# One plain run of 18 steps around the second norm, and whole tiles for the products of the FFN

## The chip, the cores and the metric

The kernel runs on one core of a Trainium2 chip. The metric is the device time of one execution in microseconds. A profiled execution also has a span, from its first to its last instruction, which lies a little below its time.

## The reference

One transformer block over 2048 rows of width 512, in float32. The vector `c` gives six modulation vectors. The block is attention with 32 heads of width 16, then a SwiGLU FFN of inner width 1792, each behind a normalization without weights.

```
mod = (_silu(c) @ w_mod).reshape(c.shape[0], 6, 1, -1)
sa, ca, ga, sb, cb, gb = (mod[:, 0], mod[:, 1], mod[:, 2], mod[:, 3], mod[:, 4], mod[:, 5])
h = _layernorm(x, axis=-1) * (1 + ca) + sa
x = x + ga * _A_ref(h, A_wqkv, A_wo)
h = _layernorm(x, axis=-1) * (1 + cb) + sb
x = x + gb * _B_ref(h, B_w_gate, B_w_up, B_w_down)
```

`_A_ref` is softmax attention over all 2048 keys followed by the product with `wo`; `_B_ref` is `(silu(x @ w_gate) * (x @ w_up)) @ w_down`.

## The kernel before

The 2048 rows are four **chunks** of 512 queries, the 32 heads eight groups of four. A chunk with a group is a **unit** of attention, 32 in all, chunk by chunk; a unit has 16 **steps**, one for each block of 128 keys, so there are 512 steps. The first three chunks (0 to 2) run the rest of their block (output product, second norm, FFN) while the attention of the next chunk goes on; the last chunk's rest comes behind all attention. The change touches the part in which both run.

A step is four **pairs** (`pair_of`). A pair is a score matmul (`score`, L573), whose result ScalarE turns into exponentials (L575), and a matmul for the row maxima of the keys of 20 steps later (`max_one`, L524), whose result VectorE reduces (L526). The two matmuls of a pair use the two row halves of TensorE. Every 16 steps a unit's maxima are complete; they are then written as two extra rows into its `qop`, with which the first score of that unit, 16 pairs later, is made. That is done in one of two ways. `max_rows` reduces (L531), makes three small matmuls (L536 to L538) two windows later and sends two DMAs (L542). `max_turned` reduces (L549), works on VectorE (L554, L556) and sends eight small DMAs on SyncE's queue (L563); its parts are hung, one each, behind the next five pairs. The flag `beside` says which: false in plain runs, true in tiles.

The product of exponentials and values, PV, comes in halves of a step (`pv_step`, L588), made in groups by `pvs`, one step behind the scores. After the last half of a unit, `close_unit` sends its sums on and loads keys and queries for the unit three later.

TensorE's order is written out by two functions:

- `plain(steps, tails)` runs pairs without FFN work. A **window** is three pairs, then a tail if there is one for this window, then one or two PV halves after the pattern `HALVES`, then the work whose turn in the list `behind` has come (`turns_behind` counts down once a window). The maxima take turns on four PSUM banks; a tail takes one of the same four. Each call begins that order of banks anew.
- `filled_tile(job, ...)` puts the matmuls of an FFN product between pairs. With the order `FOUR`, 16 pairs and all 24 pieces of work are one stretch, behind which all PV halves follow; the product's row halves then trade banks in the middle. Where the tile would start on a unit's last step (`one` is false), it is cut into two calls with the order `TWO`, eight pairs each and its own PV group behind each. A down product (`DOWN`) is eight pairs.

For chunk `ci` the program is: plain up to step `STARTS[ci]`; the two output products; the norm run; 14 gate-and-up tiles (`gate_up`) and 14 down tiles (`down`) in the order of `ch.jobs`. The norm run begins with the sums of the second norm on ScalarE (`minus_mean` L829, `squares` L833), put into `behind` by `add_o`; then `scaled` (three VectorE operations, L746 to L748, 13 small GpSimd ones and four normalizing ones, L768); then four tails `ch.turned` (four transposes L773 into one bank, evacuated by ScalarE in L775, split by GpSimd in L776 and L777), whose results the first gate tile reads. Before the change the run is `plain(9)` with tails in its last three windows and `plain(3)` with the fourth in its first; chunk 2 adds 18 plain steps there and six before its gate tile 7. Chunks 0 and 1 have three plain steps ahead of their last pair of down tiles, (6, 0) and (6, 2). What remains up to the next `STARTS` is plain. Weights come on SyncE's queue, one gate weight of 1 MB for each tile (L718) and one down weight of 1 MB for each pair of tiles (L723).

Of the kernel before, what the change touches and what calls it, by code (L numbers as in the profile page):

```python
# [28 lines left out]
NK = D // P  # L29
# [4 lines left out]
NF = F // P  # L34
FG = 2
# [6 lines left out]
WIN = 3  # L42
# [3 lines left out]
PTS = 5  # L46
FBANKS = (3, 6)
KEEP = 7
REST = 18
NORM = 9  # L50
STARTS = (147, 275, 403)
TWO = (0, 3, 2, 2, 2, 2, 1, 0)
DOWN = (0, 3, 3, 0, 3, 3, 0, 0)
# [51 lines left out]
def block_kernel(ctx, tc, x, wqkv, wo, w_gate, w_up, w_down, c, w_mod, out):  # L105
# [391 lines left out]
    posts, behind = [], []  # L497
# [134 lines left out]
    def tile_mid():  # L632
        return pf.tile([P, 2, CW], F32R, name="mid", tag="mid", bufs=3)

    def tmp(name):
        return pf.tile([P, CW], F32, name=name, tag="tmp", bufs=4)
# [177 lines left out]
    def add_o(ch, t0, outs, late):  # L814
        if ch.mv is None:
            ch.mv = pf.tile([P, 4, 2], F32, name="mv2", tag="mv2", bufs=1)
            ch.rs = pf.tile([P, 4], F32, name="rs", tag="rs", bufs=1)
            ch.rs2 = pf.tile([P, 2, 4], F32, name="rs2", tag="rs2", bufs=1)
        for e in range(2):
            t = t0 + e  # L820
            nc.vector.tensor_add(ch.x2[:, t, :], outs[e], ch.x2[:, t, :])

        def sums(t):
            st = pf.tile([P, 6], F32, name="stt", tag="stt", bufs=2)
            nc.vector.bn_stats(st, ch.x2[:, t, :])
            nc.vector.bn_aggr(ch.mv[:, t, :], st)

        def minus_mean(t):
            nc.scalar.activation(tmp("sq"), ch.x2[:, t, :], AF.Identity, scale=-1.0 / D,  # L829
                                 accum_out=ch.mv[:, t, 0:1])  # L830

        def squares(t):
            nc.scalar.activation(tmp("sq"), ch.x2[:, t, :], AF.Square, bias=ch.mv[:, t, 0:1],  # L833
                                 accum_out=ch.mv[:, t, 1:2])

        if late:
            turns = (1, 1, 2, 2) if t0 == 0 else (1, 2, 3, 4)
            works = ((minus_mean, t0), (squares, t0), (minus_mean, t0 + 1), (squares, t0 + 1))
            behind.extend([k, lambda f=f, t=t: f(t)] for k, (f, t) in zip(turns, works))
        else:  # L840
            for e in range(2):
                sums(t0 + e)

    def out_pair(ch, t0, outs, halves, trade=False):
        return accumulate(outs, lambda e, a, k: ch.oT[a][:, k, (t0 + e) * P:(t0 + e + 1) * P],
                          lambda b, k: ch.wo[k // 2][:, b, k % 2, :], NK,
                          lambda: posts.append(lambda: add_o(ch, t0, outs, True)), halves, trade=trade)
# [60 lines left out]
    def scaled(ch):  # L908
        ch.load_gu(0)
        ch.norm_scale(nc.gpsimd)  # L910
        ch.nt = [tile_mid().bitcast(F32) for _ in range(2)]
        for t in range(4):
            ch.normalize(t)
# [40 lines left out]
    beside = True  # L954
# [28 lines left out]
    def pair_of():  # L983
        nonlocal done
        i = done // 4 - 1
        most = 4 * n - 4 * (LEAD - 1)
        h = (ORDER if done < most else (0, 1, 2, 3))[done % 4]
        work = [lambda: score(i + 1, h)]
        if done < most:
            work.insert(1 - h % 2, lambda: max_one(done + 4 * (LEAD - 1)))  # L990
        for f in work:
            f()
        done += 1
        if side:
            side.pop(0)()
# [22 lines left out]
    def pvs(most, by_halves):  # L1018

        nonlocal owed  # L1020
        if by_halves:
            most, owed = most + owed, 0
        while most and halves and 4 * halves[0][0] + 8 <= done:
            i, half = halves.pop(0)
            pv_step(i, half)
            most -= 1
            if i % 16 == 15 and half:
                close_unit(i // 16, done // 4 - 1)
                if by_halves:
                    break  # L1030
        if by_halves and most and halves and 4 * halves[0][0] + 8 <= done:
            owed = most

    def turns_behind():
        for b in list(behind):
            b[0] -= 1
            if not b[0]:
                b[1]()
                behind.remove(b)

    def end_steps():
        nonlocal ended
        while ended < done // 4:
            after(ended - 1)
            ended += 1

    def plain(steps, tails=()):

        nonlocal four, bank, beside
        beside = False  # L1050
        assert steps % WIN == 0 and done % 4 == 0
        four, bank = Turn(0, 3, 1, 2), Turn(4, 5, 6)
        for w in range(4 * steps // WIN):
            for _ in range(WIN):
                pair_of()
            if w < len(tails) and tails[w]:
                tails[w](four())
            pvs((HALVES[(w - 2) % 4] if done > 8 else 0) + (w == 4 * steps // WIN - 1), True)
            turns_behind()
            end_steps()  # L1060

    def filled(places, work):

        nonlocal four, bank, beside
        beside = True
        four, bank = three, Turn(4, 5)
        if done >= 4 * n - 4 * (LEAD - 1):
            places, bank = ALONE.get(places, places), Turn(4, 5, 0, 1, 2)
        for r in range(len(places)):
            pair_of()  # L1070
            take(work, places[r])
            if r % 4 == 3:
                end_steps()
        hook()
        pvs(len(places) // 2 + 2, False)
        turns_behind()

    def filled_tile(job, ch, arg):
        one = done // 4 % 16 != 15 and done + 16 <= 4 * n - 4 * (LEAD - 1)
        work = job(ch, arg, outs, True, one)  # L1080
        for places in (FOUR,) if one else (TWO, TWO):
            filled(places, work)
# [14 lines left out]
    for ci in range(last):  # L1097
        plain(STARTS[ci] - done // 4)
        ch = chunks[ci]
        for t0 in (0, 2):  # L1100
            filled_tile(out_pair, ch, t0)
        behind.append([4, lambda: scaled(ch)])
        tails = [lambda tp, k=k: ch.turned(tp, k) for k in range(NK)]
        plain(NORM, [None] * NORM + tails[:3])
        plain(WIN, tails[3:])
        if ci == last - 1:
            plain(REST)
        for _ in range(len(ch.jobs) - (KEEP if ci == last - 1 else 0)):
            job, args = ch.jobs.pop(0)
            if args == (NF // FG - 1, 0):  # L1110
                plain(WIN)
            if ci == last - 1 and args == (7,):
                plain(24 - REST)
            if job is gate_up:
                filled_tile(job, ch, *args)
            else:
                filled(DOWN, job(ch, *args, outs, True))
# [5 lines left out]
    turns = chain([2, 3, 2, 0, 1, 2, 0], cycle([1, 3, 2, 0]))  # L1123
# [19 lines left out]
    ch, chp = chunks[last], chunks[last - 1]  # L1143
# [10 lines left out]
    for t in range(4):  # L1154
        out_terms(ch, t, banks[t], (NK - 1,))
        if t % 2:
            add_o(ch, t - 1, banks[t - 1:t + 1], False)
# [40 lines left out]
```

## Time and profile before

| | before |
|---|---|
| time, median of 3 runs | 1821.43 us (1820.22 to 1823.81) |
| time of the profiled execution | 1822.87 us |
| its span | 1821.1 us |
| granted clock of TensorE, mean | 0.999 |
| costliest VectorE line, L526 | 1259.7 us busy, 2048 reduces |
| chain that ended last | PE 96%, DVE 2%, ACT 2% |

The busy shares of the page are averages over the whole span, and matmul ends are modelled, so TensorE's share says little about a single stretch. The view of windows gives the busy time and the number of instructions of each engine within chosen stretches; the timeline lists an engine's instructions in order, merged where they follow each other, with the idle time before them and its releaser in brackets.

### The profile page before, as it was taken

What the parts mean: (1) busy time and instruction counts of PE and PEld (TensorE: products, weight loads), DVE (VectorE), ACT (ScalarE), POOL (GpSimd) and SP (SyncE); (2) the same over time, 40 slices, a digit from 0 to 9 for tenths busy, and PEclk for the clock granted to TensorE, in tenths of its full rate; (3) what the DMA queues carried; (4) which work ended last, traced back from release to release, by engine and by line L of the source; (5) the groups of instructions that cost most, each with busy time, mean ns of one, the idle gap of its engine ahead of it and who ended that gap; (6) DMA issues with size and microseconds to landing.
All of it is one profiled execution on the core that took longest, in us unless ns stands there. A gap on an engine that the chain in (4) does not pass through costs nothing.

```text
span 1821.1 us, 41022 instructions
## 1 busy us (share of the span) xinstructions
PE 1809.9 (99%) x16898; PEld 1181.1 (65%) x16898; DVE 1507.0 (83%) x2556; ACT 1234.9 (68%) x2357; POOL 459.9 (25%) x538
## 2 busy tenths in 40 slices
PE   9999999999999999999999999999999999999999
PEld 6876444444455777776565777776564677667887
DVE  5568999999999888888999888888989988922544
ACT  4222888888888666767888676676888867773211
POOL 3612544456323111111123111111113111031200
PEclk9999999999999999999999999999999999999999
DMA  8873866666845444553554554444643565233742
GB/s 290 306 220 133 208 182 201 167 178 192 217 81 124 106 114 141 125 149 69 136 122 109 129 130 119 126 119 89 163 80 57 126 149 121 106 122 118 286 167 103
DMA packets 80596, 267.63 MB, mean 147 GB/s; under 512 B 19744, under 2 KB 24320, under 8 KB 59728
## 3 DMA queue, kind: packets, MB, share of 16 engines
q1 hardware_dynamic: 61432, 179.71, 34.0%
q0 software_dynamic: 18288, 84.49, 19.5%
q8 instruction: 133, 2.18, 0.5%
q10 hardware_dynamic: 688, 0.80, 0.1%
q14 instruction: 55, 0.45, 0.1%
HBM read 201.85 MB, written 62.13 MB: 145 GB/s over the span
## 4 chain that ended last, share of the span: by engine, by line
PE 96%; DVE 2%; ACT 2%; DMA 0%; issue 0%; SPq 0%; DVEq 0%; ACTq 0%
PE bank L588 26%; PE bank L790 20%; PE bank L573 18%; PE bank L524 15%; PE bank L809 8%; PE bank L214 7%; DVE mx L526 2%; PE bank L852 1%; PE bank L773 0%; DMA wm_ab<-in_w_mod 0%; PE bank L166 0%; ACT sq L833 0%; PE bank L538 0%; DVE v_flat L883 0%; PE bank L537 0%
## 5 line engine op out<-in xcount | busy, mean ns | idle before, releaser
L526 DVE TENSOR_REDUCE mx<-bank 128x1 f32<-128x512 f32 x2048 | 1259.7, 680 | 118.4 <-PE bank L524 84.8
L573 PE MATMUL bank<-qop,kop 50*128 50x512 f32 x2048 | 732.2, 427 | 0.6 <-ACT pu__17793 L575 0.2
L524 PE MATMUL bank<-kop,qop 48*128 48x512 f32 x2048 | 726.3, 425 | 0.3
L573 PEld LDWEIGHTS bank<-qop,kop 50*128 50x128 f32 x2048 | 345.5, 184 | 192.0 <-issue 37.4
L524 PEld LDWEIGHTS bank<-kop,qop 48*128 48x128 f32 x2048 | 345.2, 184 | 107.3 <-DVE mx L526 62.5
L790 PE MATMUL bank<-act,wgu 64*128 64x512 f32 x1872 | 306.6, 392 | 0.0
L790 PEld LDWEIGHTS bank<-act,wgu 64*128 64x128 f32 x1872 | 194.0, 187 | 17.6
L614 POOL TENSOR_TENSOR rb<-o,rb 128x512 f32<-128x512 f32 x31 | 39.9, 1286 | 539.1 <-DMA rb<-d_dr 363.2
L790 PE MATMUL bank<-wd,mid 64*128 64x512 f32 x912 | 131.5, 391 | 0.0
L871 POOL CAST mid<-m 128x512 fp32r<-128x512 f32 x40 | 24.4, 611 | 347.6 <-DVE m L869 347.6
L790 PEld LDWEIGHTS bank<-wd,mid 64*128 64x128 f32 x912 | 91.3, 186 | 11.9
L214 PE MATMUL bank<-hT,wqs 128*128 128x512 f32 x384 | 94.5, 397 | 0.6 <-DVE wqs L354 0.4
L214 PEld LDWEIGHTS bank<-hT,wqs 128*128 128x128 f32 x384 | 70.6, 188 | 19.4 <-issue 3.1
L867 DVE SCALAR_TENSOR_TENSOR q<-th,bank 128x512 f32<-128x512 f32 x56 | 38.1, 680 | 54.2 <-ACT th L863 54.2
L863 ACT ACTIVATE th<-bank 128x512 f32<-128x512 f32 x56 | 33.4, 597 | 57.9 <-PE bank L809 57.9
L883 DVE TENSOR_TENSOR x<-bank,x 128x512 f32<-128x512 f32 x84 | 53.9, 685 | 16.2 <-PE bank L790 16.1
L869 DVE TENSOR_TENSOR m<-bank,q 128x512 f32<-128x512 f32 x56 | 38.7, 692 | 21.7 <-PE bank L809 19.7
L872 POOL TENSOR_TENSOR mid<-m,mid 128x512 fp32r<-128x512 f32 x40 | 51.4, 1285 | 3.3
L809 PE MATMUL bank<-wd,mid 128*128 128x512 f32 x216 | 51.3, 393 | 0.0
L214 PE MATMUL bank<-wqs,hT 128*128 128x512 f32 x192 | 47.9, 397 | 0.0
L790 PE MATMUL bank<-wgu,act 64*128 64x512 f32 x288 | 47.8, 392 | 0.0
L809 PEld LDWEIGHTS bank<-wd,mid 128*128 128x128 f32 x216 | 40.4, 188 | 8.9
(6300 smaller groups left out, 5142.7 us busy)
## 6 DMA issues: line engine op xcount, KB each, us to landing
wgu<-gu_dr SPq DMA_DIRECT2D x48, 1024.0 KB
wd<-wd_dr SPq DMA_DIRECT2D x28, 1024.0 KB
kop<-kd SPq DMA_DIRECT2D x33, 768.0 KB
kop<-kd POOLq DMA_DIRECT2D x29, 768.0 KB, 8.6
gu_dr<-wgu POOLq DMA_DIRECT2D x14, 1024.0 KB, 12.7
kd<-prt SPq DMA_DIRECT2D x16, 512.0 KB
qd<-prt SPq DMA_DIRECT2D x16, 512.0 KB
kop<-gu_dr SPq DMA_DIRECT2D x8, 1024.0 KB
```

The lines of the kernel that those rows point to most:

```text
L214: nc.tensor.matmul(pt, lhs(a, k), rhs(b, k), start=(n == 0), stop=(n == 3 * nk - 1))
L524: nc.tensor.matmul(pm, qop[u][rows, s, qt * P:(qt + 1) * P], kop[u % 3][rows, s, kc * CW:(kc + 1) * CW], start=True, stop=True)
L526: nc.vector.tensor_reduce(mx[u][:, b, s, qt, kc:kc + 1], pm, op=ALU.max, axis=AX.X)
L573: nc.tensor.matmul(sp, kop[u % 3][rows, h // 2, kt * P:(kt + 1) * P], qop[u][rows, h // 2, :], start=True, stop=True)
L588: nc.tensor.matmul(pv[u][32 * h:32 * h + 32, cols], v_flat[:, e0:e0 + 32], p_[h][:, cols], start=(kt == 0 and half == 0), stop=(kt == 15), ...
L614: mul.tensor_mul(rb, o, rb)
L790: mm = nc.tensor.matmul(outs[e], lhs(e, a, k)[rows], rhs(b, k)[rows], start=(ph == 0 and j == 0), stop=(j == z and (ph == 1 or trade)), sk ...
L809: nc.tensor.matmul(outs[e], lhs(e, a, k), rhs(b, k), start=(j == 0), stop=(j == z))
L867: nc.vector.scalar_tensor_tensor(q, th, 1.0, outs[0], op0=ALU.add, op1=ALU.mult)
L869: nc.vector.tensor_mul(m32, outs[1], q)
L872: (nc.gpsimd if slow else nc.vector).tensor_sub(mid[:, 1, :], m32, mid[:, 0, :].bitcast(F32))
L883: nc.vector.tensor_add(ch.x2[:, t, :], outs[e], ch.x2[:, t, :])
```

## The change

The 9 and 3 steps of the norm run, with tails in windows 9, 10, 11 and 12, become one call of 18 steps (24 windows) with tails in windows 10, 13, 16 and 19, counted from 0. The second output product's sums come in windows with other counts, and `scaled` waits six turns in place of four. The three steps ahead of the last down tiles are gone. Chunk 2's extra steps are 12 in place of 18, so that its norm run and extra steps are 30 in all as before. The runs that lead to `STARTS` shrink by themselves, from 21 to 18 steps. In the last two windows of a plain call `beside` is true.

```diff
-REST = 18
-NORM = 9
+REST = 12
+NORM = 18
...
-            turns = (1, 1, 2, 2) if t0 == 0 else (1, 2, 3, 4)
+            turns = (1, 1, 2, 2) if t0 == 0 else (1, 1, 2, 4)
...
         for w in range(4 * steps // WIN):
+            beside = w > 4 * steps // WIN - 3
...
-        behind.append([4, lambda: scaled(ch)])
-        tails = [lambda tp, k=k: ch.turned(tp, k) for k in range(NK)]
-        plain(NORM, [None] * NORM + tails[:3])
-        plain(WIN, tails[3:])
+        behind.append([6, lambda: scaled(ch)])
+        tails = [None] * 10
+        for k in range(NK):
+            tails += [lambda tp, k=k: ch.turned(tp, k), None, None]
+        plain(NORM, tails)
         if ci == last - 1:
             plain(REST)
...
-            if args == (NF // FG - 1, 0):
-                plain(WIN)
             if ci == last - 1 and args == (7,):
-                plain(24 - REST)
+                plain(18 - REST)
```

How the instructions stand now is shown at three places. The first is ScalarE in the norm run of chunk 0, from the first tail to the third before, and from the first to the second now; L775 evacuates a tail's bank, L575 makes one pair's exponentials. Before:

```order
L775 ACTIVATE h_6596<-bank_64,modc 128x512
L575 ACTIVATE pt__6611<-bank_68 128x512
L575 ACTIVATE pu__6616<-bank_69 128x512
L575 ACTIVATE pt__6619<-bank_67 128x512
L775 ACTIVATE h_6628<-bank_64,modc 128x512
L575 ACTIVATE pt__6640<-bank_68 128x512
L575 ACTIVATE pt__6647<-bank_69 128x512
L575 ACTIVATE pu__6652<-bank_67 128x512
L775 ACTIVATE h_6659<-bank_64,modc 128x512
```

The same place on ScalarE now:

```order
L775 ACTIVATE h_6620<-bank_66,modc 128x512
L575 ACTIVATE pt__6632<-bank_68 128x512
L575 ACTIVATE pt__6639<-bank_69 128x512
L575 ACTIVATE pu__6644<-bank_67 128x512
L575 ACTIVATE pt__6651<-bank_68 128x512
L575 ACTIVATE pt__6656<-bank_69 128x512
L575 ACTIVATE pt__6663<-bank_67 128x512
L575 ACTIVATE pu__6672<-bank_68 128x512
L575 ACTIVATE pt__6675<-bank_69 128x512
L575 ACTIVATE pt__6680<-bank_67 128x512
L775 ACTIVATE h_6689<-bank_65,modc 128x512
```

Nine pairs, three windows, lie between two tails where there were three pairs, and the tails take turns on the banks of the maxima (bank_63 to bank_66) in another order.

The second is TensorE in the middle of chunk 0's gate tile 2, at the end of its first 12 pieces (L790; bank_66 and bank_69 are its two results). Before:

```order
L790 MATMUL bank_66<-act_1608,wgu 128x512
L790 MATMUL bank_69<-act_1608,wgu 128x512
L524 MATMUL bank_65<-kop_88,qop 128x512
L573 MATMUL bank_68<-qop,kop_1508 128x512
L588 MATMUL bank_70<-pt__7061,v_flat 32x256
L588 MATMUL bank_70<-pt__7079,v_flat 32x256
L588 MATMUL bank_70<-pt__7070,v_flat 32x256
L588 MATMUL bank_70<-pu__7090,v_flat 32x256
```

The same place on TensorE now:

```order
L790 MATMUL bank_66<-act_1608,wgu 128x512
L790 MATMUL bank_69<-act_1608,wgu 128x512
L524 MATMUL bank_65<-kop_88,qop 128x512
L573 MATMUL bank_68<-qop,kop_1508 128x512
L573 MATMUL bank_67<-qop,kop_1508 128x512
L524 MATMUL bank_63<-kop_88,qop 128x512
L790 MATMUL bank_69<-act_1608,wgu 128x512
L790 MATMUL bank_66<-act_1608,wgu 128x512
```

The PV group (L588) that stood in the middle of the tile is gone from there, and the second row half follows with its two banks traded.

The third is SyncE's queue around chunk 0's gate tile 3, where the maxima of unit 12 are sent (L563); L599, L604 and L609 belong to closing a unit, L448 loads keys and queries. Before:

```order
L723 DMA wd<-wd_dr 128x2048
L718 DMA wgu<-gu_dr 128x2048
L604 DMA d_dr<-dn 128x16
L609 DMA rb<-d_dr 128x1x512
L718 DMA wgu<-gu_dr 128x2048
L563 DMA qop<-turned 2x8x32 x8
L599 DMA dn<-o 128x1x16
```

The same place on SyncE's queue now:

```order
L718 DMA wgu<-gu_dr 128x2048 x2
L604 DMA d_dr<-dn 128x16
L609 DMA rb<-d_dr 128x1x512
L723 DMA wd<-wd_dr 128x2048
L718 DMA wgu<-gu_dr 128x2048
L563 DMA qop<-turned 2x8x32 x8
L599 DMA dn<-o 128x1x16
```

The eight small DMAs stood behind one gate weight and the closing of a unit, and stand now directly behind a down weight and a gate weight.

## The prediction

> **What bounds the kernel now.** The page first. TensorE looks like the bound, since its modelled ends count it busy nearly throughout:
>
> ```profile
> PE 1809.9 (99%) x16898; PEld 1181.1 (65%) x16898; DVE 1507.0 (83%) x2556; ACT 1234.9 (68%) x2357; POOL 459.9 (25%) x538
> ```
>
> An average over two regimes hides what matters, so I cut the span by the scheduler's own calls. Each stretch below starts at the first score matmul (L573) of its call in TensorE's timeline; the view of windows then gives length, busy time and count of each engine.
>
> ```profile
> core 0: us, PE busy (x) PEld busy (x) DVE busy (x) ACT busy (x) POOL busy (x), PEclk, DMA share, GB/s
> 556.06:588.45 32.39, 31.96 (x315) 15.97 (x311) 29.52 (x52) 29.66 (x61) 14.30 (x27) 1.00 0.52 91
> 858.20:865.61 7.41, 7.41 (x76) 3.45 (x72) 6.83 (x13) 5.99 (x12) 0.67 (x1) 1.00 0.03 4
> 879.53:930.29 50.76, 50.57 (x514) 24.29 (x510) 50.60 (x87) 44.60 (x88) 14.05 (x19) 1.00 0.64 155
> 1390.42:1434.50 44.08, 43.76 (x442) 21.23 (x438) 43.49 (x76) 38.35 (x76) 3.03 (x4) 1.00 0.35 59
> 615.49:629.09 13.60, 13.60 (x149) 10.40 (x146) 11.32 (x18) 10.11 (x18) 1.99 (x3) 1.00 0.83 150
> 642.67:655.99 13.32, 13.32 (x148) 9.64 (x144) 11.51 (x20) 9.23 (x17) 1.48 (x2) 1.00 0.59 224
> ...
> 957.39:989.76 32.37, 31.96 (x315) 16.00 (x311) 29.51 (x52) 29.66 (x61) 14.28 (x27) 1.00 0.52 90
> 1259.12:1266.52 7.40, 7.40 (x76) 3.47 (x72) 6.83 (x13) 5.99 (x12) 0.69 (x1) 1.00 0.02 2
> 1280.11:1331.23 51.12, 50.91 (x514) 24.69 (x511) 50.53 (x87) 44.64 (x88) 14.05 (x19) 1.00 0.66 157
> 1358.07:1390.42 32.35, 31.93 (x314) 16.00 (x310) 29.50 (x52) 29.64 (x61) 15.39 (x29) 1.00 0.45 72
> ```
>
> In order: chunk 0's norm run (9+3 steps), its 3 steps ahead of the last down tiles, the 21 steps after, chunk 2's 18 extra steps, a gate tile cut in two (g2 of chunk 0), a whole tile (g3); then chunk 1's norm run, its 3 and its 21 steps, and chunk 2's norm run. A plain run of 84 pairs takes 50.76, and VectorE is busy 50.60 of it. Its timeline there is one unbroken chain:
>
> ```profile
> 878.67 19.56 DVE L526 TENSOR_REDUCE mx<-bank 128x1 f32<-128x512 f32 x32
> ...
> 898.31 16.16 DVE L526 TENSOR_REDUCE mx<-bank 128x1 f32<-128x512 f32 x27
> 914.39 0.21 DVE L531 TENSOR_REDUCE m<-mx 128x16 f32<-128x64 f32 x1
> 914.52 16.22 DVE L526 TENSOR_REDUCE mx<-bank 128x1 f32<-128x512 f32 x27
> ```
>
> 16.22/27 is 0.60 us a reduce: **plain steps are bound by VectorE**, 1.80 a window of three pairs. Tiles are bound by TensorE (13.32 of 13.32). The norm run is neither: 48 reduces are 28.8 of its 32.39. Its VectorE timeline shows the holes in brackets:
>
> ```profile
> 556.64 3.68 DVE L526 TENSOR_REDUCE mx<-bank 128x1 f32<-128x512 f32 x6 [2.13 <-PE bank L524]
> 560.24 0.21 DVE L531 TENSOR_REDUCE m<-mx 128x16 f32<-128x64 f32 x1
> 560.36 1.87 DVE L526 TENSOR_REDUCE mx<-bank 128x1 f32<-128x512 f32 x3
> 562.40 1.89 DVE L526 TENSOR_REDUCE mx<-bank 128x1 f32<-128x512 f32 x3 [0.16 <-PE bank L573]
> 564.20 0.16 DVE L746 TENSOR_SCALAR mv<-mv 128x4 f32<-128x4 f32 x1
> ...
> 564.85 10.97 DVE L526 TENSOR_REDUCE mx<-bank 128x1 f32<-128x512 f32 x18
> 576.27 1.89 DVE L526 TENSOR_REDUCE mx<-bank 128x1 f32<-128x512 f32 x3 [0.45 <-PE bank L573]
> 578.78 1.89 DVE L526 TENSOR_REDUCE mx<-bank 128x1 f32<-128x512 f32 x3 [0.62 <-PE bank L524]
> 581.27 3.68 DVE L526 TENSOR_REDUCE mx<-bank 128x1 f32<-128x512 f32 x6 [0.60 <-PE bank L524]
> 585.17 4.53 DVE L526 TENSOR_REDUCE mx<-bank 128x1 f32<-128x512 f32 x7 [0.22 <-PE bank L573]
> ```
>
> Check: 0.58 to the first reduce, 47 x 0.60 to the start of the 48th, 0.12 for L531, 0.65 for L746 to L748 make 29.55; so 2.84 is waiting. The five brackets behind the first are 2.05, and 2.45 with the 0.08 by which rows overlap in the unbroken chain; the other 0.39 is smaller holes and the way from the last reduce to the next tile. The holes from 576 on follow the four turns (L773), which stand in four windows in a row:
>
> ```profile
> 575.74 0.50 PE L573 MATMUL bank<-qop,kop 50*128 50x512 f32 x1
> ...
> 576.63 0.66 PE L773 MATMUL bank<-ident,mid 128*128 128x128 f32 x4
> 577.22 0.40 PE L588 MATMUL bank<-pt__6550,v_flat 128*32 128x256 f32 x1
> ...
> 577.67 0.38 PE L588 MATMUL bank<-pt__6550,v_flat 128*32 128x256 f32 x1
> ...
> 578.22 0.49 PE L573 MATMUL bank<-qop,kop 50*128 50x512 f32 x1
> ```
>
> A window from 575.74 to 578.22 takes TensorE 2.48; the turn is 0.59 of it (576.63 to 577.22), a PV half 0.45 (577.22 to 577.67). So without a turn it needs 1.89 with two halves and 1.44 with one. Against VectorE's 1.80 TensorE loses 0.09 in the first kind and gains 0.36 in the second: spread out, half of the windows can absorb a turn; bunched, none can.
>
> **The change, part by part.** *The norm run, 18 steps, 72 pairs.* VectorE needs 0.58 + 71 x 0.60 + 0.12 (L531) + 0.12 (the same reduce for the second unit, L549) + 0.65 = 44.07; for the way to the next tile I allow 0.16. Then the waits. The first turn today costs TensorE 0.68 (0.59 + 0.09) and leaves a hole of 0.45, 0.53 with the overlap; so TensorE's usable lead is 0.15, and it is refilled by any one-half window. The turns now stand in windows 10, 13, 16, 19, of which the first two have two halves and the others one. Window by window: 0.53 (10), 0 (11, 12), 0.53 (13), 0.09 (14), 0 (15), 0.08 (16), 0.09, 0.09, 0.23 (19), 0 (20), 0.12 (21 to 23): 1.76. The hole of 0.16 (0.24) behind the first run of maxima stays, so 2.0 and a run of **46.2**. Ends: no wait but that one, 44.5; the turns at their old price, 32.39 + 24 x 0.60 + 0.12 = 46.9. I take 46.2, near the upper end, since it is that price worked through. ScalarE's sums (L829, L833) move by a window; ScalarE is busy 29.66 of 32.39 and is awaited by nobody there, so nothing. A new wait is possible: the turns need all four normalized rows, and `scaled` now comes two windows later while the first turn moves one.
>
> ```profile
> 568.61 3.04 POOL L768 TENSOR_SCALAR mid<-x,rs,rs 128x512 f32<-128x512 f32 x4
> ```
>
> GpSimd ends at 571.65, 7.45 behind L746 at 564.20. From the end of window 5 to the turn lie four windows and three pairs, 4 x 1.80 + 0.89 = 8.1. It holds by 0.6, if VectorE is no further behind there; if it is, up to 0.6 a run.
>
> *Chunks 0 and 1.* Gone are the 3 steps ahead of the down tiles, and the 21 steps become 18 (12 pairs, 7.2 less). Chunk 0: 32.39 + 7.41 + 50.76 = 90.56 becomes 46.2 + 43.56: -0.8. Chunk 1: 90.89 becomes 46.2 + 43.92: -0.8.
>
> *Chunk 2.* 18 extra steps become 12. One more hole goes:
>
> ```profile
> 1391.57 0.69 DVE L526 TENSOR_REDUCE mx<-bank 128x1 f32<-128x512 f32 x1 [0.59 <-PE bank L524]
> ```
>
> A plain call begins its turn of banks anew; the 3-step call before it uses 13 banks (12 pairs, a turn) and so ends on the one with which the next begins. The new run uses 76, a whole number of fours. So 44.08 - 14.4 - 0.67 (0.59 and the overlap) - 0.12 (L531, now in the run before) = 28.9, and 32.35 + 44.08 = 76.43 becomes 75.1: -1.3.
>
> *Tiles.* Shifted by six steps, no tile of chunks 0 and 1 starts on a unit's last step, so the three of each chunk that were cut in two (13.60 above) become whole (13.32): 0.28, the two PV groups in one. Six of them: -1.7. A whole tile in which a unit closes isn't dearer: 13.34 in a row below.
>
> **Sum**: -0.8 - 0.8 - 1.3 - 1.7 = -4.6. The profiled execution has a span of 1821.1 and took 1822.87; it becomes 1816.5 and 1818.3. Its time lies 1.44 above the median of the three, 1821.43, from which 4.6 makes **1816.8**.
>
> Every turn costs a change from row halves to the full array and back. The Trainium skill, TensorEngine Tiling (Array Packing), Key Properties, says "Mode switching requires drain". By that rule a turn costs the same in any window, spreading would bring nothing, and the sum would be the second rival's. The trace agrees on the price (0.59 each time), and shows besides who pays: VectorE waits only where TensorE's lead is used up.
>
> **Rivals.** *The waits vanish*: one-half windows refill more than 0.15. For it: in the 84-pair run the 27 reduces from 914.52 stay unbroken although the three small matmuls L536 to L538 come between. Against: a turn takes one of the maxima's four banks, those do not. Three runs at 44.5 to 45.5: 1811.7 to 1814.7.
>
> *Turns keep their price*: 46.9 a run, 0.7 x 3 = 2.1 less gained: 1818.9. For it: two of the turns still stand in two-half windows, and GpSimd's rows may come late.
>
> *Late rows, slower.* In chunks 0 and 1 four turned maxima (eight small DMAs) now stand on SyncE's queue behind a down weight and a gate weight.
>
> ```profile
> 608.17 4.38 SPq L563 DMA_DIRECT2D qop<-turned  x8
> ...
> 640.83 0.42 SPq L718 DMA_DIRECT2D wgu<-gu_dr  x1
> ```
>
> ```profile
> 650.14 0.43 PE L573 MATMUL bank<-qop,kop 50*128 50x512 f32 x1
> ```
>
> ```profile
> 640.40:647.40 7.00, 7.00 (x76) 4.91 (x74) 6.68 (x13) 4.94 (x9) 0.00 (x0) 1.00 0.81 303
> ```
>
> These two loads move 303 GB/s x 7 us, 2.1 MB, until 647.4, 4.7 into the tile that starts at 642.67; the 13th score, which needs the rows, runs 7.5 into it (650.14). If the rows start only behind the loads, they end 4.7 + 4.4 = 9.1 in, 1.6 late, and with 2.4 to land (estimate, from the page's 2.4 for GpSimd's 256 KB to o_dr) 4.0 late: four times, 16, 1833. It decides from 2.1 late each. The eight of the norm run's second unit are milder: they start some 1.5 into the first gate tile (0.58, a reduce, two small VectorE steps), end at 5.9 and are there by 8.3 at most: 0 to 0.8 late in two tiles; I take 0. Against it: in chunk 2 the rows already stand behind a gate load, and the tile is whole and no longer:
>
> ```profile
> 1445.67 5.40 SPq L563 DMA_DIRECT2D qop<-turned  x8
> ```
>
> ```profile
> 1447.88:1461.22 13.34, 13.34 (x148) 9.47 (x145) 11.21 (x18) 9.24 (x17) 2.46 (x3) 1.00 0.06 23
> ```
>
> That the change does not do what it says is excluded by the rows in the part on the change.
>
> **How the numbers follow.** Forecast 1815 to 1818.5: 0.55; waits vanish: 0.17; turns keep their price: 0.19; late rows: 0.09. The range is 1812.5 to 1820.5: it takes in the second and third and most of the first. A measurement tells about 0.2% (3.6 us, 1817.8) from no change. Faster: 0.17 + 0.44 of the forecast + 0.03 = 0.64; same: 0.11 + 0.16 + 0.02 = 0.29; slower: 0.07 of the late rows.
>
> **What would show it.** VectorE's holes in a norm run should sum to about 2.0, the largest two behind windows 10 and 13; the run should be 46.2, the 18 steps after a chunk 43.6 to 43.9, the 12 extra steps 28.9 without a hole at their start; every tile of chunks 0 and 1 about 13.3. Wrong if the holes sum to 2.8 (turns at full price), if TensorE waits for `qop` at the 13th pair of a tile, or if L773 waits for GpSimd's L768.

## The result, and the profile after

| | before | after |
|---|---|---|
| time, median of five runs each, side by side | 1822.70 us | **1848.96 us** (1848.19 to 1851.23) |
| ratio, 95% interval | | 1.015 (1.0135 to 1.0164) |
| span of the profiled execution | 1821.1 us | 1849.3 us |
| granted clock, mean | 0.999 | 0.991 |

The change makes the kernel 1.5% slower. The forecast was 0.3% faster, and the time lies far outside its range.

The page of after names what is new. From its chain of work that ended last (shares by engine, then by line), and from its costliest groups (busy time, mean ns | idle before, with the releaser):

```profile
PE 79%; DVE 14%; DMA 5%; ACT 1%; issue 0%; SPq 0%; DVEq 0%; ACTq 0%
...
L790 PE MATMUL bank<-act,wgu 64*128 64x512 f32 x1872 | 314.7, 402 | 21.5 <-DMA wgu<-gu_dr 21.5
```

The same group on the page of before, whose chain has DMA at 0%:

```profile
L790 PE MATMUL bank<-act,wgu 64*128 64x512 f32 x1872 | 306.6, 392 | 0.0
```

DMA stands in the chain now, and the matmuls that read a gate weight have waited 21.5 us for it. TensorE's waits of after (total, times, longest) count four such waits:

```profile
PE bank L790 <- DMA wgu<-gu_dr: 21.5, 4, 5.7
```

They lie in gate tiles 2 and 10 of chunks 0 and 1. The view of windows over these four tiles (columns as in the prediction: length, busy time of PE, PEld, DVE, ACT and POOL, granted clock, DMA share, GB/s):

```profile
628.61:649.60 20.99, 15.74 (x148) 11.39 (x144) 11.59 (x19) 9.35 (x17) 1.88 (x3) 0.84 0.34 116
797.50:819.53 22.03, 16.35 (x148) 11.91 (x144) 11.67 (x19) 9.43 (x17) 1.79 (x3) 0.77 0.29 105
1044.44:1065.70 21.26, 16.02 (x148) 11.71 (x144) 11.59 (x19) 9.44 (x17) 1.80 (x3) 0.84 0.34 116
1214.42:1236.03 21.61, 16.30 (x149) 11.93 (x145) 11.69 (x19) 9.44 (x17) 1.81 (x3) 0.84 0.30 106
```

A whole tile should take 13.32; these take 85.89 in all, 32.6 too much, of which only 21.5 is waiting. The rest shows in TensorE's timeline of the first of them (start, duration, last the idle time before with its releaser), and in windows that cut it at the end of the wait and at 640:

```profile
634.60 1.65 PE L790 MATMUL bank<-act,wgu 64*128 64x512 f32 x6 [5.25 <-DMA wgu<-gu_dr]
636.02 0.62 PE L524 MATMUL bank<-kop,qop 48*128 48x512 f32 x1
...
639.95 0.39 PE L524 MATMUL bank<-kop,qop 48*128 48x512 f32 x1
```

```profile
628.61:634.60 5.99, 0.74 (x9) 0.33 (x6) 1.29 (x2) 1.08 (x2) 0.70 (x1) 0.84 0.99 334
634.60:640.00 5.40, 5.40 (x28) 4.54 (x30) 2.14 (x4) 1.89 (x4) 0.00 (x0) 0.54 0.09 36
640.00:649.60 9.60, 9.60 (x116) 6.53 (x112) 8.16 (x14) 6.37 (x12) 1.18 (x2) 1.00 0.07 24
```

Behind 5.25 us of idleness the granted clock is 0.54 for some 5 us, and the same matmul takes 0.62 in place of 0.39. So a tile pays the wait and then, on the mean of the four, some 2.8 of half-speed work: (32.6 - 21.5) / 4.

Why the weight is late is read from the queues. SyncE's and GpSimd's timelines of after, around the end of gate tile 0:

```profile
615.95 0.60 SPq L599 DMA_DIRECT2D dn<-o  x1
616.66 0.42 SPq L448 DMA_DIRECT2D kop<-kd  x1
617.16 0.38 SPq L448 DMA_DIRECT2D qop<-qd  x1
617.64 7.58 SPq L718 DMA_DIRECT2D wgu<-gu_dr  x2
```

```profile
615.85 0.58 POOL L448 DMA_DIRECT2D kop<-kd  x1
```

Unit 10 is closed in the PV group at the end of gate tile 0. `close_unit` sends the unit's sums (L599) and loads keys and queries for the unit three later (L448), half on each queue, 768 and 192 KB each; GpSimd's queries follow its keys at 616.41. Only behind them does gate tile 1, at its start, ask for the weight of tile 2 (L718, 617.64), and tile 2 starts at 628.61. Before, the same queue had it the other way round:

```profile
598.37 0.31 SPq L718 DMA_DIRECT2D wgu<-gu_dr  x1
...
623.01 0.61 SPq L599 DMA_DIRECT2D dn<-o  x1
623.71 0.42 SPq L448 DMA_DIRECT2D kop<-kd  x1
```

There unit 10 closed in the middle of the cut tile 2, and the weight of tile 2 had been asked for 25 us ahead of SyncE's half of the keys. The cut tiles that the change abolished were the places where a closing could do no harm.

What the keys cost shows in windows of after that hold GpSimd's half of the keys (617.10 on) and SyncE's half (621.90 on):

```profile
617.10:622.70 5.60, 5.60 (x50) 4.28 (x48) 5.50 (x9) 4.88 (x9) 0.00 (x0) 1.00 1.03 160
621.90:627.80 5.90, 5.90 (x80) 4.04 (x80) 5.33 (x9) 4.01 (x8) 0.46 (x1) 1.00 1.01 167
```

The DMA engines are full (share 1.03 and 1.01), yet move 160 to 167 GB/s, about half of the 303 at which the weights ran in the prediction's row. Two halves with their queries are 1.97 MB and so take some 12 us, until about 629. A weight behind them is late for a tile that starts at 628.6.

### The profile page after: what moved, and what is told of

It reads as the page before. It is cut to its first block, busy times and chain, and to the rows that moved or that the text cites. A ratio compares the mean times of both kernels' runs of the same rounds, so it can differ in the third digit from the quotient of the medians.

```text
span 1849.3 us, 41033 instructions
## 1 busy us (share of the span) xinstructions
PE 1815.8 (98%) x16892; PEld 1180.7 (64%) x16892; DVE 1508.7 (82%) x2558; ACT 1234.1 (67%) x2356; POOL 459.3 (25%) x538
## 4 chain that ended last, share of the span: by engine, by line
PE 79%; DVE 14%; DMA 5%; ACT 1%; issue 0%; SPq 0%; DVEq 0%; ACTq 0%
PE bank L588 20%; PE bank L790 19%; DVE mx L526 14%; PE bank L573 13%; PE bank L524 11%; PE bank L809 8%; PE bank L214 7%; DMA wgu<-gu_dr 4%; PE bank L852 1%; DMA dn<-o 1%; DMA wm_ab<-in_w_mod 1%; PE bank L773 0%; PE bank L166 0%; DVE v_flat L883 0%; ACT o L592 0%
## 5 line engine op out<-in xcount | busy, mean ns | idle before, releaser
L524 PE MATMUL bank<-kop,qop 48*128 48x512 f32 x2048 | 728.5, 427 | 1.0 <-DVE mx L526 0.5
L524 PEld LDWEIGHTS bank<-kop,qop 48*128 48x128 f32 x2048 | 348.8, 186 | 111.1 <-DVE mx L526 67.6
L790 PE MATMUL bank<-act,wgu 64*128 64x512 f32 x1872 | 314.7, 402 | 21.5 <-DMA wgu<-gu_dr 21.5
L790 PEld LDWEIGHTS bank<-act,wgu 64*128 64x128 f32 x1872 | 195.9, 192 | 42.4 <-issue 23.1
L790 PE MATMUL bank<-wd,mid 64*128 64x512 f32 x912 | 131.1, 391 | 0.0
L790 PEld LDWEIGHTS bank<-wd,mid 64*128 64x128 f32 x912 | 91.0, 186 | 12.1
L790 PE MATMUL bank<-wgu,act 64*128 64x512 f32 x288 | 47.8, 392 | 0.0
```

Source lines behind the costliest of these rows:

```text
L524: nc.tensor.matmul(pm, qop[u][rows, s, qt * P:(qt + 1) * P], kop[u % 3][rows, s, kc * CW:(kc + 1) * CW], start=True, stop=True)
L790: mm = nc.tensor.matmul(outs[e], lhs(e, a, k)[rows], rhs(b, k)[rows], start=(ph == 0 and j == 0), stop=(j == z and (ph == 1 or trade)), sk ...
```

## The experiments

Each is the changed kernel with one edit, except where the kernel before is named. Kernels of one batch ran on one chip beside the kernel before: 1823.37 for the first four, 1820.63 for the next four (one run), 1821.59 for the last four. Only two of them were run more than once: the first, six times, and the one called the same line in the kernel before, ten times. The runs of before lie between 1820.2 and 1825.8, so a few microseconds in the time of a single run say nothing; the lengths of tiles and runs in its trace say more.

**The weight ahead of the closing.** A tile's last matmul frees a weight buffer; the next weight is asked for there, and not at the start of the tile that follows the closing.

```diff
@@ gate_up, after()
             posts.append(later)
+            if halves:
+                ch.load_gu(f + 2)
```

> The changed kernel, with each gate weight's DMA written right behind the last matmul of the tile that frees its buffer, so ahead of the closing of a unit (DMA of its sums, keys and queries three units on) on SyncE's queue. Theory A (order: the weights of gate tiles 2 and 10 of chunks 0 and 1 stand behind a closing, are issued 6 us late and land behind 2 MB of keys): the four long tiles return to 13.3, 32.6 us less than 1849, so 1816.5. Theory B (these two tiles are the ones that the change made whole, and the whole form is dear there): no change, 1849. Theory C (keys and weights collide in the DMA engines in whatever order they are queued): part of the 32.6 remains, time above 1825.

Measured: **1816.76** (1816.11 to 1818.17, six runs), ratio to before 0.9969 (0.9956 to 0.9981). SyncE's timeline at the same place, and gate tile 2 of chunk 0 in the view of windows:

```profile
610.06 0.33 SPq L718 DMA_DIRECT2D wgu<-gu_dr  x1
614.53 0.61 SPq L599 DMA_DIRECT2D dn<-o  x1
615.19 0.46 SPq L448 DMA_DIRECT2D kop<-kd  x1
```

```profile
627.16:640.46 13.30, 13.30 (x148) 9.65 (x144) 11.28 (x19) 9.24 (x17) 1.87 (x3) 1.00 0.48 134
```

The weight leaves 5.1 ahead of the keys, the tile takes 13.30 at full clock, and no matmul waits for a gate weight. This one line takes back the whole loss and beats both kernels.

**The long tiles cut in two.** Tiles 2 and 10 of chunks 0 and 1 in the old form of two halves.

```diff
+        cut = job is gate_up and ch.ci < last - 1 and arg in (2, 10)
-        one = done // 4 % 16 != 15 and done + 16 <= 4 * n - 4 * (LEAD - 1)
+        one = not cut and done // 4 % 16 != 15 and done + 16 <= 4 * n - 4 * (LEAD - 1)
```

> The changed kernel, with gate tiles 2 and 10 of chunks 0 and 1 cut in two calls again, as they were before the change. Theory A: the weight still comes late, the four tiles stay at 21 to 22 and lose 0.3 each: 1850. Theory B: the four tiles return to 13.6: 1818. Theory C: 1850.

Measured: 1848.75, with tiles of 22.06, 20.69, 20.64 and 20.85. The form of the tile is not the cause.

**A shift of three steps in place of six.**

```diff
-REST = 12
-NORM = 18
+REST = 15
+NORM = 15
...
-                plain(18 - REST)
+                plain(21 - REST)
```

> The changed kernel with a norm run of 15 steps (chunk 2's extra steps 15, so that the total stays), so that every tile of chunks 0 and 1 starts three steps earlier against the units. Theory A: closings now fall at the end of tile 1, tile 4, the down tiles (2, 2), tile 9 or 10 and tile 12; only behind the one at (2, 2) do two gate tiles follow, so tiles 2 and 10 return to 13.3 and tile 8 takes 21 to 22 in both chunks: two long tiles in place of four, 1833. Theory B: tiles 2 and 10, still whole, stay long: 1849. Theory C: some tile behind each closing is long, at a place that follows the closings; as A if only bytes count.

Measured: 1831.17, near the number by luck, for another reason. The long tiles that were expected did not come (13.55 and 14.01). TensorE's waits show what came instead:

```profile
PE bank L588 <- ACT o L592: 7.1, 10, 0.7
```

With this shift units close inside a PV group, and the next unit's first PV half waits for ScalarE's copy of the bank, ten times. Four gate tiles of each of chunks 0 and 1 in which that happens take 14.2 in place of 13.4. The ten waits are 7.1 of the 14.4 by which this run lies above the first experiment's; the rest was not followed up. A closing can hurt in a second way; in the changed kernel it doesn't.

**All keys on GpSimd's queue.** If the order on SyncE's queue were all, this would free the weight.

```diff
@@ load_k
-        load_parts(kop[u % 3], kd, u % NG, 0, S, nc.gpsimd if u > 2 else nc.sync)
+        load_parts(kop[u % 3], kd, u % NG, 0, S, nc.gpsimd if u > 2 else nc.sync, nc.gpsimd if u > 2 else nc.sync)
@@ load_q
-        first, second = [(nc.gpsimd, nc.sync)[k] for k in ((0, 0), (1, 1), (1, 0))[min(u, 1) + (u > 2)]]
+        first, second = [(nc.gpsimd, nc.sync)[k] for k in ((0, 0), (1, 1), (0, 0))[min(u, 1) + (u > 2)]]
```

> The changed kernel with all keys and queries of a closing issued by GpSimd's queue, none by SyncE's; the same bytes at about the same moment, the weight behind the closing's sums alone on SyncE. Theory A, its byte part as a queue's own order: the weight overtakes the keys, lands in 5 to 6 us, the four tiles return to 13.3: 1817. Theory B: 1849. Theory C: the four tiles stay long by some 4 to 8 each: 1832 to 1849.

Measured: 1873.21. TensorE's waits:

```profile
PE bank L790 <- DMA wgu<-gu_dr: 11.8, 3, 4.2
```

The weight now stands behind no keys on its own queue and is still late in three tiles (19.00, 19.20 and 18.54; the fourth takes 14.17). The rest of the loss lies elsewhere: the 18 steps after chunks 0 and 1 take 50.89 and 52.12 in place of 43.7, and everything up to the first output tile some 20 more. The maxima's matmuls (L524) wait there, 15.7 in seven waits; what they wait for was not followed up. The theory of queue order falls: a queue of its own does not keep the weight clear of the keys. This agrees with the Trainium skill, DMA: Bandwidth & Descriptors, Rules for kernel authors: spreading transfers over issuing engines brings no bandwidth, since all of them run on the same 16 DMA engines.

**The tails bunched.** The first experiment's kernel, with its four tails in windows 10 to 13.

```diff
-        tails = [None] * 10
-        for k in range(NK):
-            tails += [lambda tp, k=k: ch.turned(tp, k), None, None]
+        tails = [None] * 10 + [lambda tp, k=k: ch.turned(tp, k) for k in range(NK)]
```

> The changed kernel with the weights ahead as in the first experiment, and the four turns in windows 10 to 13 in place of 10, 13, 16 and 19. If spreading saves what the prediction says (0.7 of a run's waits), the three norm runs are 47.2 in place of 46.5 and the time is 2.1 above the first experiment's 1816.8: 1819. If a turn has one price wherever it stands, the runs stay 46.5: 1817.

Measured: 1818.76 beside a before of 1820.63, one run each. The three norm runs take 46.29, 46.27 and 46.26, against 46.55, 46.53 and 46.53 with spread tails; the next tile takes 13.79 and 13.60 in chunks 0 and 1 against 13.51 and 13.32. Run and tile together are the same in these two chunks, 60.08 and 60.06 in chunk 0. VectorE's timeline of the bunched run:

```profile
577.71 1.89 DVE L526 TENSOR_REDUCE mx<-bank 128x1 f32<-128x512 f32 x3 [0.48 <-PE bank L524]
579.76 3.90 DVE L526 TENSOR_REDUCE mx<-bank 128x1 f32<-128x512 f32 x6 [0.17 <-PE bank L524]
584.26 7.41 DVE L526 TENSOR_REDUCE mx<-bank 128x1 f32<-128x512 f32 x12 [0.60 <-PE bank L573]
```

Four turns in a row cost 1.25 here, where before they cost 1.89 (0.45, 0.62, 0.60 and 0.22). Spreading the turns is worth nothing in one long call.

**SyncE's half of the keys behind the weight.**

```diff
@@ close_unit
-            load_k(u + 3)
-            load_q(u + 3)
+            at(i + 2, lambda: load_k(u + 3))
+            at(i + 2, lambda: load_q(u + 3))
```

> The changed kernel with the keys and queries of a closing written two steps later: on SyncE's queue they then stand behind the weight, which still waits for the closing's sums and so starts only 1 us earlier; GpSimd's half of the keys stays where it is. Theory D (bytes: the 16 engines work the bytes off in the order of their issue, whatever the queue, and the weight lands when all issued before it are through): half of the bytes are gone from ahead of the weight, and the waits shrink by about half, to 3 to 5 in each of the four tiles: 1829 to 1837. Theory A2 (the wait for the closing's sums alone makes the weight late): 7 each, 1845.

Measured: 1821.19, tiles 2 and 10 at 13.68, 14.12, 13.70 and 14.23, one wait for a weight of 0.7. SyncE's timeline:

```profile
615.57 0.60 SPq L599 DMA_DIRECT2D dn<-o  x1
616.27 0.42 SPq L718 DMA_DIRECT2D wgu<-gu_dr  x1
616.74 0.42 SPq L448 DMA_DIRECT2D kop<-kd  x1
```

The weight leaves 12.0 ahead of its tile (616.27 to 628.23), in the changed kernel 11.0 (617.64 to 628.61), and the tile gets 7.3 shorter (20.99 to 13.68). What left its way is one half of the keys, some 6 us of the engines' time. At the weights' 303 GB/s a half would be 3.2 us, and 1 to 2 us of each wait would have stayed; the remainder was expected larger than it is.

**Half of the keys.** From the fourth unit on, a closing loads only the first 1024 keys; the other columns stay from an earlier unit, so the attention is another one.

```diff
-        load_parts(kop[u % 3], kd, u % NG, 0, S, nc.gpsimd if u > 2 else nc.sync)
+        to = S // 2 if u > 2 else S
+        load_parts(kop[u % 3][:, :, 0:to], kd, u % NG, 0, to, nc.gpsimd if u > 2 else nc.sync)
```

> The changed kernel that loads only the first 1024 of the 2048 columns of keys at each closing; the rest of the keys is left as the buffer's earlier unit had it. All instructions of the engines stay. Theory D: 0.77 MB less ahead of the weight, 4 to 5 us, so the four tiles wait 3 to 4 each in place of 8: 1831. Theory A2: the weight is issued as late as before, 8 each, 1849.

Measured: 1819.5. Tiles 2 and 10 take 13.32, 13.31, 13.30 and 13.30, though every transfer is issued in the changed kernel's order. What is moved ahead of the weight decides, not the order alone. Half of the keys is 0.79 MB, some 5 us at 160 to 167 GB/s, about as long as the waits that went; again the remainder was expected too large.

**The sums sent by ScalarE.** The weight then doesn't stand behind L599, which waits for the last PV half.

```diff
@@ close_unit
-        res[u] = out_a(u, nc.sync)
+        res[u] = out_a(u, nc.scalar)
```

> The changed kernel with the closing's small DMA of sums (dn) issued by ScalarE, which makes those sums, so that SyncE waits no longer for the last PV half: its half of the keys goes out 5 us earlier, and the weight behind it when its buffer is free, 6 us earlier. Theory A2: the four tiles are 13.3 again: 1817. Theory D: the bytes ahead of the weight are now one half of the keys, done by about the tile's start, and GpSimd's half is behind it: also near 1817, at most 1 each: 1817 to 1821. Theory B or a port that is simply too slow for all these bytes: above 1830.

Measured: 1851.51. TensorE's waits, and SyncE's timeline ahead of tile 10 of chunk 0:

```profile
PE bank L790 <- DMA wgu<-gu_dr: 9.2, 2, 4.8
```

```profile
780.44 0.33 SPq L723 DMA_DIRECT2D wd<-wd_dr  x1
780.81 0.43 SPq L448 DMA_DIRECT2D kop<-kd  x1
781.34 0.38 SPq L448 DMA_DIRECT2D qop<-qd  x1
781.76 11.65 SPq L718 DMA_DIRECT2D wgu<-gu_dr  x2
```

Tile 2 is cured (13.32): its weight leaves at 615.50 behind SyncE's half of the keys alone, since GpSimd's half is issued only at 619.86. Tile 10 isn't (20.16 and 20.25): its weight leaves 15.0 ahead of the tile (781.76 to 796.80), in the changed kernel 11.0 ahead (786.49 to 797.50), and is late all the same, with GpSimd's half (778.82), a down weight and SyncE's half ahead of it. Issued 4.0 earlier behind the same bytes, it lands so little sooner that the wait goes from 5.7 to 4.4. The 18 steps after a chunk take 46.4 in place of 43.7: in those after chunk 0 TensorE waits 0.8 for ScalarE, and the granted clock is 0.51 from 902.50 to 905.90, which costs some 1.7.

**The same line in the kernel before.** The first experiment's two lines, added to before.

> The kernel before, with the one line that brought the changed kernel to 1816.8: the weight of a gate tile is loaded right behind the last matmul of the tile whose buffer it takes, ahead of the closings' keys. Bytes ahead (mine: the loss needs a closing ahead of a gate weight whose tile follows within some 12 us; in the kernel before the closings fall into the cut tiles, and no tile there waits for its weight): nothing to gain, 1821.5 to 1823.5, every tile of chunks 0 and 1 as before (13.3, the cut ones 13.6). Rival (the weight's early load is worth something by itself, so that the 6 us that the changed kernel gained with it say nothing of the norm runs): 1816 to 1819, some tile shorter than before by over 0.3.

Measured: 1821.33 (ten runs) beside 1821.59, ratio 0.9995 (0.9986 to 1.0005), and every tile of chunks 0 and 1 within 0.05 of before. The early weight has no worth of its own; the gain of the first experiment is the change's.

**The shift alone.** The kernel before, with only the six steps moved.

```diff
-REST = 18
+REST = 12
...
+            beside = w > 4 * steps // WIN - 3
...
-        plain(WIN, tails[3:])
+        plain(9, tails[3:])
...
-            if args == (NF // FG - 1, 0):
-                plain(WIN)
             if ci == last - 1 and args == (7,):
-                plain(24 - REST)
+                plain(18 - REST)
```

> The kernel before, with only the six steps moved ahead of the gate tiles (9 and 9 steps around the second norm, none ahead of the last down tiles, the late run of chunk 2 shortened by as much); the four sums and transposes bunched as before and in two calls. Bytes ahead (mine: the shift alone makes the loss): gate tiles 2 and 10 of chunks 0 and 1 take 20 to 22, weights are waited for 20 to 23 in all, 1848 to 1852. Rival (the loss needs the one run of eighteen steps, with its sums spread and its later scaling, which puts the first weight's load and the chain behind it later): no wait for weights, 1818 to 1822.

Measured: 1851.80, and the same four waits:

```profile
PE bank L790 <- DMA wgu<-gu_dr: 21.4, 4, 5.6
```

Tiles 2 and 10 take 20.64, 21.60, 20.94 and 21.64. The shift makes the loss, without the one run, the spread tails or the later scaling. The 2.8 above the changed kernel (one run against five) are in the main chunk 2's 12 extra steps, 31.17 in place of 29.02, and most of that is a stretch of half clock:

```profile
1436.30:1439.70 3.40, 3.40 (x30) 1.40 (x26) 2.84 (x6) 1.42 (x4) 0.00 (x0) 0.50 0.02 4
```

**The next weight later.** Tiles 2 and 10 of chunks 0 and 1 ask for the following tile's weight at their end.

```diff
@@ gate_up
-        ch.load_gu(f + ch.ahead)
+        wait = ch.ci < last - 1 and f in (2, 10)
+        if not wait:
+            ch.load_gu(f + ch.ahead)
...
             posts.append(later)
+            if wait:
+                ch.load_gu(f + ch.ahead)
```

> The changed kernel, but gate tiles 2 and 10 of chunks 0 and 1 ask for the weight of the next gate tile at their end, not ahead of their start, so that it doesn't share the DMA engines with their own weight. Sharing (mine: of the 5 to 6 us that such a tile waits some 3.5 are the next weight's bytes, read from the packets of both weights that come interleaved): waits of 1 to 2.5 each, 4 to 10 in all, the granted clock of these tiles stays at 1.00, 1823 to 1832. Rival (the weight is late by the keys ahead of it alone; the next weight's packets stand behind it): the tiles stay at 20 to 22 and the time at 1847 to 1851.

Measured: 1849.90. TensorE's timeline in tile 2 of chunk 0:

```profile
635.33 1.65 PE L790 MATMUL bank<-act,wgu 64*128 64x512 f32 x6 [5.90 <-DMA wgu<-gu_dr]
```

The wait isn't shorter (22.5 in all against 21.5): the weight is late by the keys ahead of it, and what comes behind it does it no harm. The theory of sharing, mine, falls. With one weight alone behind the keys, the way is plain in the windows of this kernel: GpSimd's half, SyncE's half, and later a weight that has the engines to itself.

```profile
617.10:621.50 4.40, 4.40 (x40) 3.35 (x37) 4.30 (x8) 3.85 (x7) 0.00 (x0) 1.00 1.04 168
623.20:627.70 4.50, 4.50 (x66) 2.98 (x66) 4.11 (x7) 2.90 (x6) 0.28 (x1) 1.00 1.09 175
647.20:650.60 3.40, 3.40 (x65) 1.92 (x64) 2.18 (x4) 0.95 (x2) 1.04 (x2) 1.00 0.88 314
```

Keys move at 168 to 175 GB/s with the engines full, a weight at 314 with room left.

**The shift undone.** One run of 12 steps with its tails in windows 10 to 13, three steps ahead of the last down tiles, 18 in chunk 2 as before; the later scaling and the other turns stay.

```diff
-REST = 12
-NORM = 18
+REST = 18
+NORM = 12
...
-        tails = [None] * 10
-        for k in range(NK):
-            tails += [lambda tp, k=k: ch.turned(tp, k), None, None]
+        tails = [None] * 10 + [lambda tp, k=k: ch.turned(tp, k) for k in range(NK)]
...
+            if args == (NF // FG - 1, 0):
+                plain(WIN)
             if ci == last - 1 and args == (7,):
-                plain(18 - REST)
+                plain(24 - REST)
```

> The changed kernel with the shift undone: one run of 12 steps around the second norm, its four sums and transposes in windows 10 to 13, three steps ahead of the last down tiles and 18 steps in chunk 2's run as before; the later scaling and the other turns stay. Bytes ahead (mine): no tile waits for a weight, the tiles are those of the kernel before, three of them cut in each chunk; one norm run of 12 steps in place of 9 and 3 gains some 0.8 each: 1819 to 1822. Rival (the later scaling brings the loss): gate tiles over 18, 1835 to 1850.

Measured: 1819.61, no wait for a weight. The norm run of 12 steps takes 31.90 where 9 and 3 took 32.39: one call in place of two, with the later scaling and the other turns in it, is worth 0.49.

## Why the prediction was wrong

The terms of the runs between the tiles came out smaller than forecast by 0.2 to 0.5 each, and in the cured kernel that of the tiles as it stood. The windows of after, in the order of the kernel: norm run and 18 steps of chunk 0, the same of chunk 1, then norm run and 12 extra steps of chunk 2.

```profile
555.16:601.68 46.52, 45.97 (x458) 22.19 (x454) 44.60 (x78) 41.73 (x85) 16.22 (x29) 1.00 0.52 120
900.44:944.15 43.71, 43.45 (x442) 20.92 (x438) 43.36 (x75) 38.52 (x76) 13.90 (x18) 1.00 0.69 175
971.22:1017.72 46.50, 45.95 (x458) 22.21 (x454) 44.57 (x78) 41.82 (x86) 16.21 (x29) 1.00 0.50 118
1316.94:1360.71 43.77, 43.57 (x442) 20.98 (x438) 43.18 (x75) 38.52 (x76) 13.87 (x18) 1.00 0.67 173
1387.55:1434.05 46.50, 45.96 (x458) 22.21 (x454) 44.59 (x78) 41.82 (x86) 16.10 (x30) 1.00 0.38 79
1434.05:1463.07 29.02, 28.65 (x289) 13.71 (x289) 28.62 (x51) 25.11 (x49) 1.25 (x3) 1.00 0.49 79
```

| step | predicted | after | cured |
|---|---|---|---|
| chunk 0: norm run and 18 steps | -0.8 | 90.56 to 90.23: -0.3 | same |
| chunk 1 | -0.8 | 90.89 to 90.27: -0.6 | same |
| chunk 2: norm run and 12 steps | -1.3 | 76.43 to 75.52: -0.9 | same |
| six tiles made whole, 13.60 to 13.3 | -1.7 | two at -0.3, four at +7.4 to +8.4 | six at -0.3 |

"Cured" is the first experiment's kernel. Together its terms are -3.6, and the span of before differs from that kernel's by 6.2; it was measured 5.7 faster (0.31%, 0.19 to 0.44), and of the profiled spans the rest lies ahead of the first output tile, where executions of one and the same part differ by up to 2.6.

*The step that failed* is the one on the tiles: "Shifted by six steps, no tile of chunks 0 and 1 starts on a unit's last step, so the three of each chunk that were cut in two (13.60 above) become whole (13.32): 0.28, the two PV groups in one", with "A whole tile in which a unit closes isn't dearer". It looked at the tile in which a unit closes. It didn't follow what the closing issues: of the DMAs that move with a closing, the rival of the late rows priced eight small ones, and left out 1.97 MB of keys and queries, which moved from behind the weight of tile 2 to ahead of it. The part on the change shows the order of SyncE's queue only from the two gate weights on (L718 x2, the weights of tiles 2 and 3); the closing's keys stand directly ahead of that row. The runs show the price: 32.6, against the -1.7 of the term. The shift alone makes it, the order of weight and keys alone removes it, and half of the keys removes it as well.

Even with the keys in the sum, the figure at hand would have misled. At 303 GB/s, the only pace of a load that the prediction works out, 1.97 MB of keys and 1.05 MB of weight take 10 us, and from the first issue at 615.85, with 1.3 until the first byte (617.1), all would have landed around 627, ahead of the tile at 628.6. At the keys' own pace it is 12 and 3.5, and the same 1.3: around 633, with the wait measured until 634.60. The page of before had the pace, in its row of DMA issues: 768 KB of keys from GpSimd took 8.6 us to land.

*The rivals.* "Late rows, slower" had the right kind (a transfer on SyncE's queue that lands behind its tile's need) and the wrong transfer. The rows came in time: the view of TensorE's waits of after lists none for `qop`.

*The turns.* The run of 46.2 came at 46.5, and the holes in it came where and as large as they were worked out. VectorE's timeline of after:

```profile
576.94 5.47 DVE L526 TENSOR_REDUCE mx<-bank 128x1 f32<-128x512 f32 x9 [0.47 <-PE bank L524]
582.80 7.53 DVE L526 TENSOR_REDUCE mx<-bank 128x1 f32<-128x512 f32 x12 [0.39 <-PE bank L524]
```

These stand behind windows 10 and 13, and one of 0.17 at 594.43 behind window 19. With the overlap of 0.08 they are 0.55, 0.47 and 0.25, where 0.53, 0.53 and 0.23 were forecast; together with those too small for a bracket, taken in the trace from the start of one reduce to the next, they sum to some 2.0, as forecast. The 0.3 that the run took more is the way from its last reduce (601.20) to the next tile (601.68), 0.48 where 0.16 was allowed. What doesn't hold is the other side of the comparison, that spreading gains 0.7 a run. The price of bunched turns, 46.9, was taken over from two calls; in one call the bunched run takes 46.27 and gives 0.28 back in the next tile of chunks 0 and 1. What the change saves in the run is the second call: 0.49 in the run of 12 steps, with the later scaling and the other turns in it. Why a new call costs that much was put down to the order of banks and not tried by itself. GpSimd's normalized rows were in time: no wait for them ahead of a turn (L773) stands among TensorE's waits of after.

The hole at the start of chunk 2's extra steps is not gone, as predicted, but smaller: 0.37 ahead of their first reduce (1434.62 in VectorE's timeline) where it was 0.59; the steps take 29.02 against the forecast 28.9. In chunk 1 a third tile, 3, takes 14.08 in after and 13.30 in the cured kernel; a score matmul in it waits 0.5 for ScalarE, and why was not looked into.

## What to carry to other kernels

When a step moves, list every transfer that moves with it, and for each load behind it on any queue ask what stands ahead in bytes, at those transfers' own measured pace, and when the reader starts. Ask for a buffer's next load where the buffer comes free, not where the next job begins: it costs nothing where nothing competes (0.9995), and here it turned 1.015 into 0.9969. A form that looks like waste (a tile cut in two) can mark the place where a burst of transfers does no harm to a load with a deadline; it is the place that protects, not the form, since the tiles cut at the new place stay at 20.64 to 22.06.

## What the hardware showed beside that

- **The clock after a wait.** 5.25 us without a matmul left a granted clock of 0.54 over the next 5.4 us, and 5.68 us (tile 10 of chunk 0) one of 0.50 over the next 6.28. The Trainium skill, TensorE: Matmul & The Clock Gate, HAM oscillation — how this bites in real kernels, gives a rule against idle gaps of more than some 3.4 us, behind which TensorE runs at half its clock; these rows agree. So a late load costs its wait and half as much again: 21.5 became 32.6. The single wait of 0.7 that was left with SyncE's keys behind the weight drew no such stretch behind it (1.00 from 1193.20 to 1198.20).
- **Half a clock without a wait.** In the shift-alone run the granted clock was 0.50 from 1436.30 to 1439.70, though TensorE was busy for 7.91 of the 8.30 us before. Long gaps are thus not the only occasion; what brought this stretch is open.
- **Keys at half the pace.** 160 to 175 GB/s with the DMA engines at a share of 1.0, a weight 314 at 0.88. The keys go to 48 partitions a half, the weight to 128; which of their differences makes the pace was not tried.
- **One queue ahead of the other, and side by side.** L599's 8 KB, issued on SyncE's queue at 615.95, did not move while GpSimd's keys did: from 617.0 to 621.5 the DMA view of after counts GpSimd's queue alone, at 100.8% of the engines.

```profile
q0 software_dynamic: 94, 0.75, 100.8%
```

In the kernel with all keys on GpSimd's queue, the second half of the keys and the weight were issued within 1 us of each other (637.65 and 637.89), and the two moved side by side: from 643 to 650 the view counts 50.7% of the engines for GpSimd's queue and 51.6% for SyncE's.
